# Outputs kept in 32 bits and stored through SyncE's queue instead of GpSimd's casting queue

## Chip, cores and metric

One core of a Trainium2 chip runs the whole program. The metric is the device time of one execution in microseconds (us), the median over runs; lower is better.

## What is computed

Dilated and sliding-window attention over 8 batches of 576 rows and 8 heads of 64, followed by a soft mixture of experts with 32 slots (8 experts, 4 slots each):

```python
scores = scale * np.matmul(q, k.transpose(0, 1, 3, 2))          # masked: window 32, or dilation 4
attn = np.exp(scores); attn = attn / attn.sum(-1)
x = np.matmul(attn, v)                                          # to rows [4608, 512]
logits = x @ phi                                                # [4608, 32]
d = np.exp(logits - logits.max(0)); d /= d.sum(0)
slot_input = d.T @ x
for e in range(E):
    h = np.maximum(slot_input[e] @ w1[e], 0.0)                  # 512 -> 1024
    slot_out[e] = h @ w2[e]                                     # 1024 -> 512
c = np.exp(logits - logits.max(1)); c /= c.sum(1)
return (c @ slot_out).astype(np.float32)                        # [4608, 512]
```

Inputs and the output are float32 in DRAM: q, k and v have 9.44 MB each, w1 and w2 16.8 MB each, the output 9.44 MB.

## The kernel before

All loads of inputs and weights go through GpSimd (POOL) as `nc.gpsimd.dma_start`, since they turn float32 into float16 on the way. The only transfer that SyncE (SP) issues is that of a small table of masks, `cst`. The order of instructions on each engine is the order in the source (`tc.manual_schedule()`).

**Attention.** A loop over the 8 batches, software-pipelined by an order written out by hand (`ORDER`), computes scores, exponentials, masks, outputs and logits. Each batch's q, k and v are loaded two batches ahead, and when the last batch has freed the buffers, the loads of w2 follow: experts 3 and 4 whole, then columns 0 to 255 of experts 5, 6 and 7 ("first half"), then their columns 256 to 511 ("second half"), two transfers for each half of an expert (`load_w2`, L207). These last twelve transfers each read 512 KB of DRAM in runs of 1 KB.

**Experts.** With all of w1 in place, the hidden layer is computed (L596 to L611), and then `emit_so` (L627) multiplies by w2 into the PSUM tile `so`, by halves of the columns for experts 5 to 7. `gather_so` (L642) and `spread_so` (L648) bring a finished half into `so_sb`.

**Output.** `emit_fin` computes 128 rows of the output: a matmul (L654) into PSUM, and a scaling by `rrow` on the way into the SBUF tile `om`, alternately on ScalarE (ACT, L663) and VectorE (DVE, L667). `emit_batch` does this for the four blocks of a batch and issues one store (L674). For six batches the first half of the columns is done and stored while the second half of w2 is still being loaded; between these come the `emit_so` of the second half:

```python
    for b in range(NHALF):                      # NHALF = 6
        if b in (2, 3, 5):
            emit_so(1, ({2: 5, 3: 6, 5: 7}[b],))
        if b == 5:
            gather_so(1)
        emit_batch(b, 0, DH)
    spread_so(1)
    for b in range(NHALF):
        emit_batch(b, DH, DMODEL)
    for b in range(NHALF, B):
        emit_batch(b, 0, DMODEL)
```

That gives six stores of half width (512 KB of float32 each, in runs of 1 KB), six more for the second half, two of full width (1 MB, runs of 2 KB), and at the end two stores (L701, 512 KB each, runs of 2 KB) of the rows 512 to 575 of all batches, out of the tile `om_l`. PE executes in order, so the first-half fins of batches 2, 3 and 5 stand behind the `emit_so` of experts 5, 6 and 7.

A program of this kind gives each outstanding transfer one of eight slots of its issuing engine; a later transfer in the same slot first waits for the earlier one to land.

Of the kernel before, what the change touches and what calls it, by code (L numbers as in the profile page):

```python
# [9 lines left out]
FP32 = mybir.dt.float32  # L10
FP16 = mybir.dt.float16
# [4 lines left out]
B = 8  # L16
# [8 lines left out]
DMODEL = H * D  # L25
# [71 lines left out]
def kernel(  # L97
# [10 lines left out]
    nc = tc.nc  # L108
# [25 lines left out]
    w1_pool = ctx.enter_context(tc.tile_pool(name="w1p", bufs=1))  # L134
    w2a_pool = ctx.enter_context(tc.tile_pool(name="w2a", bufs=1))
# [234 lines left out]
    def et_cols(b):  # L370
        base = 384 * (b // 2)
        return (base, base + 128) if b % 2 == 0 else (base + 256, base + 192)
# [154 lines left out]
    for it in range(B + max(s for _, s in STEPS)):  # L527
        for op, stage in STEPS:
            b = it - stage
# [28 lines left out]
    h_pool = tc.alloc_tile_pool(name="hp", bufs=1)  # L558
# [55 lines left out]
    psum_e.release()  # L614
    psum_f = tc.alloc_tile_pool(name="psum_f", bufs=4, space=bass.MemoryType.PSUM)

    om = [w1_pool.tile([128, 4, DMODEL], FP16, name=f"om_{b}", tag=f"w1_{b}") for b in range(B)]
    om_l = h_pool.tile([128, B // 2, DMODEL], FP16, name="om_l", tag="om_l")
    so = psum_so.tile([128, DMODEL], FP32, name="so", tag="so")

    def emit_so(s, experts):
# [30 lines left out]
    def emit_fin(m, j, c0, c1, dst, blk):  # L652
        fp = psum_f.tile([128, DMODEL], FP32, name=f"f_{blk}_{c0}", tag="f")
        nc.tensor.matmul(  # L654
            fp[:, 0 : c1 - c0],
            ET[32 * j : 32 * j + 32, m : m + 128],
            so_sb[32 * j : 32 * j + 32, c0:c1],
            start=True,
            stop=True,
        )  # L660
        turn[0] += 1
        if turn[0] % 2:
            nc.scalar.activation(  # L663
                out=dst, in_=fp[:, 0 : c1 - c0], func=AF.Copy, scale=rrow[:, blk : blk + 1]
            )
        else:
            nc.vector.tensor_scalar(  # L667
                out=dst, in0=fp[:, 0 : c1 - c0], scalar1=rrow[:, blk : blk + 1], scalar2=None, op0=ALU.mult
            )

    def emit_batch(b, c0, c1):
        for j in range(4):
            emit_fin(et_cols(b)[0], j, c0, c1, om[b][:, j, c0:c1], 4 * b + j)
        nc.gpsimd.dma_start(  # L674
            out=out[S * b : S * b + 512].rearrange("(j p) d -> p j d", p=128)[:, :, c0:c1],
            in_=om[b][:, :, c0:c1],
        )
# [8 lines left out]
# [11 lines that stand above are left out]
# [1 line left out]
        emit_fin(et_cols(2 * pr)[1], pr, 0, DMODEL, om_l[:, pr, :], 4 * B + pr)  # L698
    rest = out.rearrange("(n e s) d -> n e s d", e=2, s=S)
    for e in range(2):  # L700
        nc.gpsimd.dma_start(  # L701
            out=rest[:, e, 512:576, :].rearrange("n i d -> i n d"), in_=om_l[64 * e : 64 * e + 64]
        )
    in_order.__exit__(None, None, None)
# [35 lines left out]
```

## Time and profile before

| | before |
|---|---|
| time, median of 3 runs | 179.43 us (179.11 to 179.47) |
| the profiled execution | 179.36 us, of which 177.5 us are the span from the first to the last instruction |
| busy: PE, DVE, ACT, POOL | 69%, 71%, 70%, 25% of the span |
| read from and written to DRAM | 62.07 MB and 9.44 MB |
| issues of `out_dram<-om` | 12 of 512 KB, 2 of 1024 KB, all from POOL |
| issues of `out_dram<-om_l` | 2 of 512 KB, from POOL |

The profile describes one execution. Its second part cuts the span into 40 slices and gives in tenths how busy each engine and the DMA engines were; "GB/s" counts the bytes as they are at the destination, so a load that turns float32 into float16 counts half of what it reads. The chain of waits is followed back from the last instruction to what released it.

### The profile page before, as it was taken

What the parts mean: (1) busy time and instruction counts of PE and PEld (TensorE: products, weight loads), DVE (VectorE), ACT (ScalarE), POOL (GpSimd) and SP (SyncE); (2) the same over time, 40 slices, a digit from 0 to 9 for tenths busy, and PEclk for the clock granted to TensorE, in tenths of its full rate; (3) what the DMA queues carried; (4) which work ended last, traced back from release to release, by engine and by line L of the source; (5) the groups of instructions that cost most, each with busy time, mean ns of one, the idle gap of its engine ahead of it and who ended that gap; (6) DMA issues with size and microseconds to landing.
All of it is one profiled execution on the core that took longest, in us unless ns stands there. A gap on an engine that the chain in (4) does not pass through costs nothing.

```text
span 177.5 us, 4765 instructions
## 1 busy us (share of the span) xinstructions
PE 122.4 (69%) x2016; PEld 79.8 (45%) x2016; DVE 126.3 (71%) x277; ACT 123.8 (70%) x268; POOL 44.5 (25%) x70
## 2 busy tenths in 40 slices
PE   0026828888888988989888988996776736688100
PEld 0015616656666657666666656764332312221000
DVE  6483999999999999799999998455131017789200
ACT  6007758999999999979999999995401117688100
POOL 7321022112112112118110005111111514556400
PEclk9999999999999997599999999789859975555555
DMA  5999999999999999999999999999999999999995
GB/s 90 211 214 211 214 212 215 215 213 217 214 213 216 212 215 212 212 216 216 216 211 215 214 215 223 211 220 220 209 216 190 196 197 224 387 347 394 405 414 142
DMA packets 21061, 40.85 MB, mean 230 GB/s; under 512 B 1328, under 2 KB 13744, under 8 KB 20400
## 3 DMA queue, kind: packets, MB, share of 16 engines
q0 software_dynamic: 20896, 40.41, 114.8%
q8 instruction: 16, 0.26, 0.5%
q1 hardware_dynamic: 144, 0.14, 0.3%
q14 instruction: 5, 0.04, 0.1%
HBM read 62.07 MB, written 9.44 MB: 403 GB/s over the span
## 4 chain that ended last, share of the span: by engine, by line
DMA 46%; ACT 23%; DVE 9%; PE 9%; POOL 4%; issue 3%; POOLq 0%; DVEq 0%; ACTq 0%
DMA w<-in_moe_w_dram 38%; DMA phi_raw<-in_moe_phi_dram 8%; ACT p L269 5%; ACT vX L240 5%; ACT xp L324 4%; PE f L654 3%; DVE qk L218 3%; DVE vT L218 3%; ACT om L663 2%; ACT xT L363 2%; PE rv L234 2%; ACT xT L365 2%; POOL w L193 2%; PE s L260 2%; ACT xd L324 1%
## 5 line engine op out<-in xcount | busy, mean ns | idle before, releaser
L269 ACT ACTIVATE p<-s 128x1920 f16<-128x1920 f32 (+1 forms) x24 | 44.5, 1854 | 10.3 <-PE s L260 10.2
L260 PE MATMUL s<-qk 32*128 32x128 f16 (+2 forms) x704 | 26.7, 295 | 18.9 <-DVE qk L218 12.0
L240 ACT COPY vX<-rv 128x768 f16<-128x768 f16 (+1 forms) x32 | 27.7, 944 | 1.7 <-PE rv L234 1.7
L324 ACT ACTIVATE xp<-o_P,rc_P 128x64 f16<-128x64 f32 x96 | 26.7, 503 | 2.5 <-DVE rc_P L315 2.5
L303 PEld LDWEIGHTS <-p 128*128 128x128 f16 (+1 forms) x480 | 22.4, 103 | 13.4 <-issue 3.9
L260 PEld LDWEIGHTS <-qk 32*128 32x128 f16 x704 | 17.3, 117 | 22.1 <-DVE qk L218 12.0
L280 DVE TENSOR_TENSOR p<-p,masks 128x1920 f16<-128x1920 f16 (+1 forms) x24 | 25.8, 1085 | 0.3
L218 DVE STREAM_TRANSPOSE qk<-rawQ 128x576 uint32<-128x576 uint32 x16 | 18.8, 1242 | 2.7 <-DMA rawQ<-in_q_dram 2.7
L234 PE MATMUL rv<-cst,vT 128*128 128x128 f16 x176 | 18.2, 250 | 3.1 <-DVE vT L218 1.8
L303 PE MATMUL o_P<-vX,p 128*128 128x65 f16 (+1 forms) x288 | 19.8, 204 | 0.7 <-DVE xd L328 0.2
L218 DVE STREAM_TRANSPOSE qk<-rawK 128x576 uint32<-128x576 uint32 x16 | 19.6, 1235 | 0.4 <-DMA rawK<-in_k_dram 0.4
L218 DVE STREAM_TRANSPOSE vT<-rawV 128x576 uint32<-128x576 uint32 x16 | 19.4, 1224 | 0.4 <-DMA rawV<-in_v_dram 0.4
L234 PEld LDWEIGHTS <-vT 128*128 128x128 f16 x176 | 13.8, 126 | 7.1 <-issue 3.7
L667 DVE TENSOR_SCALAR om<-f,rrow 128x256 f16<-128x256 f32 (+1 forms) x28 | 13.5, 518 | 3.7 <-PE f L654 2.2
L207 POOL DMA_DIRECT2D w<-in_moe_w_dram x12 | 8.9, 748 | 26.3 <-DMA w<-in_moe_w_dram 22.4
L663 ACT ACTIVATE om<-f,rrow 128x256 f16<-128x256 f32 (+1 forms) x28 | 12.8, 503 | 3.1 <-PE f L654 2.4
L654 PE MATMUL f<-so_sb,ET 32*128 32x256 f16 (+1 forms) x60 | 12.0, 420 | 3.8 <-ACT om L663 2.5
L674 POOL DMA_DIRECT2D out_dram<-om x14 | 10.4, 747 | 12.4 <-DVE om L667 7.0
L188 POOL DMA_DIRECT2D rawQ<-in_q_dram x8 | 5.1, 633 | 29.5 <-DVE rc_P L315 18.6
L363 ACT COPY xT<-rp 128x576 f16<-128x576 f16 x16 | 11.3, 876 | 1.1 <-PE rp L344 1.1
L303 PE MATMUL o_D<-vX,p 128*128 128x65 f16 x128 | 10.0, 204 | 2.5 <-DVE xp L328 1.4
L365 ACT COPY xT<-rd 128x576 f16<-128x576 f16 x16 | 10.6, 787 | 0.0
(83 smaller groups left out, 182.5 us busy)
## 6 DMA issues: line engine op xcount, KB each, us to landing
w<-in_moe_w_dram POOLq DMA_DIRECT2D x13, 1024.0 KB, 24.3
out_dram<-om POOLq DMA_DIRECT2D x12, 512.0 KB, 5.9
rawQ<-in_q_dram POOLq DMA_DIRECT2D x8, 576.0 KB, 12.6
rawK<-in_k_dram POOLq DMA_DIRECT2D x8, 576.0 KB, 11.3
rawV<-in_v_dram POOLq DMA_DIRECT2D x8, 576.0 KB, 11.4
w<-in_moe_w_dram POOLq DMA_DIRECT2D x12, 256.0 KB, 15.8
out_dram<-om POOLq DMA_DIRECT2D x2, 1024.0 KB, 8.5
out_dram<-om_l POOLq DMA_DIRECT2D x2, 512.0 KB, 9.1
```

The lines of the kernel that those rows point to most:

```text
L218: nc.vector.transpose(out=out_, in_=in_)
L234: nc.tensor.transpose(rg[:, n_t, :, c, :], rows, ident)
L240: copy(out=vX[b % 2][:, t0 : t0 + n, :, 0:D], in_=rg.rearrange("p n h c d -> p n h (c d)"))
L260: nc.tensor.matmul(sps[:, h, c0 : c0 + w], kk, qq, start=(tt == 0), stop=(tt == 1))
L269: return nc.scalar.activation(out=pt, in_=sps[:, :, 0:n], func=AF.Exp, scale=SCALE)
L280: return nc.vector.tensor_tensor(out=pt, in0=pt, in1=m, op=ALU.mult)
L303: nc.tensor.matmul(o[rows, h, :], lhs, rhs, start=(n == 0), stop=(n == len(jobs) - 1), skip_group_check=True,)
L324: nc.scalar.activation(out=dst[:, h], in_=src[:, h], func=AF.Copy, scale=rc[:, h : h + 1])
L363: copy(out=xT_t[b][:, c, :], in_=rg[:, 0:S])
L365: copy(out=xT_t[b][:, 2 + c, :].rearrange("p (i r) -> p i r", r=DIL), in_=rg[:, :, 0:SUB].rearrange("p r i -> p i r"),)
L654: nc.tensor.matmul(fp[:, 0 : c1 - c0], ET[32 * j : 32 * j + 32, m : m + 128], so_sb[32 * j : 32 * j + 32, c0:c1], start=True, stop=True,)
L663: nc.scalar.activation(out=dst, in_=fp[:, 0 : c1 - c0], func=AF.Copy, scale=rrow[:, blk : blk + 1])
```

## The change

The SBUF tiles `om` and `om_l` become float32; `om_l` takes the place of expert 0's w2 instead of one of its own. The stores then need no cast and are issued by SP (`nc.sync.dma_start`). The program as built has the same instructions in the same order on PE, ACT and DVE, but for one more wait each on ACT and DVE ahead of the first write to `om_l` (for expert 0's w2 to have been loaded). The 16 stores, each with its wait for ACT and DVE, move from the end of POOL's stream to SP's, behind the load of `cst`. SP's closing waits, ahead of the end of the program, grow from five to nine.

```diff
-    om = [w1_pool.tile([128, 4, DMODEL], FP16, name=f"om_{b}", tag=f"w1_{b}") for b in range(B)]
-    om_l = h_pool.tile([128, B // 2, DMODEL], FP16, name="om_l", tag="om_l")
+    om = [w1_pool.tile([128, 4, DMODEL], FP32, name=f"om_{b}", tag=f"w1_{b}") for b in range(B)]
+    om_l = w2a_pool.tile([128, B // 2, DMODEL], FP32, name="om_l", tag="w2_0")
...
     def emit_batch(b, c0, c1):
         for j in range(4):
             emit_fin(et_cols(b)[0], j, c0, c1, om[b][:, j, c0:c1], 4 * b + j)
-        nc.gpsimd.dma_start(
+        nc.sync.dma_start(
             out=out[S * b : S * b + 512].rearrange("(j p) d -> p j d", p=128)[:, :, c0:c1],
             in_=om[b][:, :, c0:c1],
         )
...
     for e in range(2):
-        nc.gpsimd.dma_start(
+        nc.sync.dma_start(
             out=rest[:, e, 512:576, :].rearrange("n i d -> i n d"), in_=om_l[64 * e : 64 * e + 64]
         )
```

## The prediction

> **What bounds the kernel.** I read the page first, its 40 slices above all:
>
> ```profile
> PE 122.4 (69%) x2016; PEld 79.8 (45%) x2016; DVE 126.3 (71%) x277; ACT 123.8 (70%) x268; POOL 44.5 (25%) x70
> DMA  5999999999999999999999999999999999999995
> GB/s 90 211 214 211 214 212 215 215 213 217 214 213 216 212 215 212 212 216 216 216 211 215 214 215 223 211 220 220 209 216 190 196 197 224 387 347 394 405 414 142
> DMA 46%; ACT 23%; DVE 9%; PE 9%; POOL 4%; issue 3%; POOLq 0%; DVEq 0%; ACTq 0%
> ```
>
> No compute engine is above 71%, while the DMA engines are busy in every slice. Loads run at about 214 GB/s counted in float16, that is 428 GB/s of float32 read; stores at 390 to 414 GB/s of float32 written. The chain of waits ends in the weights:
>
> ```profile
> 83.91 32.72 DMA w<-in_moe_w_dram
> 116.91 24.54 DMA w<-in_moe_w_dram
> 141.73 10.43 DMA w<-in_moe_w_dram
> 152.20 0.43 PE so L627 x3
> ```
>
> The change is in what follows, so I next took the stretches from 142 us on (after the name of the stretch and its length, busy time with instructions of PE, PEld, DVE, ACT, POOL, then clock, DMA share, GB/s):
>
> ```profile
> 142.00:148.00 6.00, 2.67 (x26) 1.06 (x25) 1.99 (x6) 2.00 (x6) 0.50 (x2) 0.67 1.45 196
> 148.00:152.20 4.20, 2.98 (x33) 0.84 (x25) 2.97 (x7) 2.73 (x7) 2.74 (x4) 0.50 1.65 276
> 152.20:160.20 8.00, 5.86 (x35) 1.88 (x35) 6.17 (x15) 6.25 (x16) 4.56 (x7) 0.50 1.84 370
> 160.20:168.50 8.30, 4.11 (x13) 0.64 (x10) 4.85 (x8) 3.96 (x7) 4.38 (x7) 0.50 1.88 400
> ```
>
> and POOL's timeline (start, length, what, wait before it):
>
> ```profile
> 141.73 0.74 POOL L207 DMA_DIRECT2D w<-in_moe_w_dram  x1 [0.58 <-DMA w<-in_moe_w_dram]
> 147.97 0.75 POOL L674 DMA_DIRECT2D out_dram<-om  x1 [5.50 <-DVE om L667]
> ...
> 154.41 0.75 POOL L674 DMA_DIRECT2D out_dram<-om  x1 [1.04 <-ACT so_sb L648]
> 157.36 3.79 POOL L674 DMA_DIRECT2D out_dram<-om  x5 [2.21 <-ACT om L663]
> ...
> 165.97 1.27 POOL L701 DMA_DIRECT2D out_dram<-om_l  x2 [0.64 <-issue]
> ```
>
> Every store is issued by 167.2, yet the trace's completion marks (16 for each transfer, one per DMA engine) say that the last lands at 176.03: nine us of stores are queued when compute ends. The marks also show two groups of engines. The last weights land at 149.58 on the first engine and at 152.16 on the last. On the slow group the marks follow each other without a hole: six first-half stores land from 153.51 to 160.20 (1.32 to 1.39 us apart), the second half from 161.46 to 168.45, the full ones at 170.98 and 173.52, `om_l` at 174.78 and 176.03. So the end is the slow engines' work, one queue, weights before stores. The last store's landing is followed by 1.5 us of closing waits.
>
> **The change part by part.**
>
> *Scaling into float32.* The 256-column forms took 473 ns on ACT and 480 on DVE, the 512-column forms 686 and 748, all from float32 PSUM. If the wider write doubled the part that grows with columns (213 and 268 ns per 256), a batch's two on each engine would cost 0.5 us more, 1.5 in place of 1.0, over the 1.31 of a store; I take zero, since DVE's 268 ns for 256 columns is one column a cycle or so, set by what it reads, and the nine us of queued stores cover what is left.
>
> *POOL loses 16 issues* (0.75 us each, 10.4 + 1.3 us). They are its last work; the last load was issued at 141.73, so nothing stands behind them: nothing gained. *SP gains them.* It is idle from 1.1 us on, and only the closing waits stand behind them. The slot waits in its stream (first-half stores none, the others for a transfer eight places earlier) have been met long before. The two added waits on ACT and DVE are for a load of long ago: some 0.03 us, hidden.
>
> *Rate.* A store's packets are runs of 1 KB: 32 per engine in 1.31 us, 41 ns each; full width 2.53 us for 32 of 2 KB, 79 ns. Loads with 1 KB read and 512 bytes written come 1.32 us apart too, so the larger side of the packet sets the price, and a store whose two sides are 1 KB should cost what it costs now. The only row for SP's queue is `cst`, 128 runs of 1,096 bytes that follow each other at 46 ns on an engine; by the two prices above (38 ns per KB and 3 more) they would take 44. So 0 to 2 ns more for each of the 480 packets an engine has: 0 to 0.96 us, all on the path. I take 0, because an uncast 8 KB packet in the trace took 322 ns and a load's packet with 8 KB read 324.
>
> *Issue.* `cst` occupied SP for 0.34 us with 128 runs, and its engines finished over 0.38 us, so runs seem to be handed out one engine after the other. A store has 512 runs: 0.34 us if the cost is fixed, 1.36 if it goes with the runs, 0.68 for `om_l` (256 runs). I take a value under 1.31 us, where the DMA still sets the pace; the upper end is a rival below.
>
> *Order.* This is the real difference. Before, the first store waits behind all weights; now it has a queue of its own and runs beside the last of them. Batch 0's output is complete at 147.42 (DVE's mark). Call L the time from there to its packets on a slow engine (`cst`: 0.94 us from issue to first packet). Weights left there then: 152.16 - 147.42 - L = 4.74 - L. If both queues get equal turns, this takes twice as long, and the weights end 4.74 - L later. The second half's first output was complete at 155.59, 3.43 us after the last weights; now at 155.59 + 4.74 - L, and its packets start L later: at 160.33 whatever L is. Before, they started at 161.46 - 1.31 = 160.15. First-half work fills the time until then: the sum of weights and stores to 160.20 is unchanged, and batch 5 (153.89 + 4.74 = 158.63 with its L) arrives before its turn, 160.20 - 1.32 = 158.88. So the cost is 0.18 us. It is zero if the loads get the larger share, and grows if the stores do. After that compute delivers a batch each 0.96 us against 1.31 for its store, so the queue fills again; the slip of up to 3.8 us in compute is under the 9 us of cover.
>
> The trace of before has no stretch with both queues loaded, so the share is unknown. The Trainium skill ("DMA: Bandwidth & Descriptors", Queues, rings and completion order) says that each engine goes round its queues packet by packet, a packet holding several descriptors; no run here shows it yet. By that rule the sum would be the 0.18 us or, where a load's packet holds more than a store's, nothing.
>
> *End.* SP's closing waits start 0.065 us apart (176.08, 176.15, 176.21); up to five more now follow the last landing, +0.33. But before, the end waited for POOL's closing drain until 176.77, 0.49 us after SP was ready at 176.28. If that drain waits for POOL's own stores, it is now early and the end gains 0.16; if not, SP's later 176.61 still hides under it: 0. I take 0.
>
> Sum against the profiled execution: 179.36 + 0.18 = 179.54, so 179.5 us. That execution lies 0.07 under the median of 179.43. About 0.2%, 0.36 us, is what a measurement of this kernel can tell from no change.
>
> **The rivals.**
>
> *SP's issue becomes the pace (slower).* If handing out 512 runs takes 1.36 us and each wait some 0.05, six second-half stores come at 1.41 instead of 1.31: +0.6 us; with the packets' 2 ns on top up to +1.6: 180.1 to 181.1. It decides from 1.31 us per issue on. For it: the spread of `cst`'s engines. Against: it is one short row at the start of the program.
>
> *The stores take more than their share (slower).* If they always went first, the stores of batches 0 to 2 (4.0 us) would go ahead of the 3.5 us of weights left at 148.6 (L = 1.2); batch 3 stands behind expert 6's weights on PE and comes too late to push in. The weights would end at 156.1 and the second half's packets start at 156.1 + 3.43 + 1.2 = 160.7: +0.6, 180.0. With batch 3's 1.32 ahead as well it would be +1.9, 181.2.
>
> *GpSimd's queue has hitches that go (faster).* The second-half store of batch 0 began 1.7 us after its outputs, where the others took 0.5; and one engine landed batch 2 1.77 us after batch 1 instead of 1.31, 0.45 that it never made up (175.64 against 176.03 at the end). Without that and with POOL's drain gone: -0.39 - 0.16, 178.8. Against: POOL's issues took 746 to 755 ns without exception, the late one lay under a backlog until 160.20, and a 16 KB packet of instructions at 161.93 fits the hitch and would stay. The Trainium skill ("SBUF — State Buffer", The single rule) has a rule that would make it so: VectorE in some modes locks GpSimd out of writing descriptors, which SP's queue avoids. The trace's constant issue times do not bear it out here.
>
> **How the numbers follow.** The forecast (equal or smaller share for the stores, DMA's pace kept) has 0.42, by its unknown packet price split into same 0.31, slower 0.08, faster 0.03; its own range is 179.2 to 180.0. SP's pace or dearer packets 0.27; greedy stores 0.13; hitches gone 0.14; the rest, 0.04, same or slower. Faster 0.17, same 0.33, slower 0.50. The range runs from the faster rival to the upper end of the first: 178.8 to 181.1.
>
> **What would show it.** Right: the last landing at about 176.2, stores 1.31 and 2.53 us apart, last weights (the last `so` of L627) 2 to 4 us later than 152.2, `om` rows at 470 to 480 ns. Wrong: SP's store rows near or above 1.3 us, a DMA slice under 380 GB/s between 161 and 168 us, `om` rows over 650 ns, or SP's stores landing before any weight moves on.

## The result

The changed kernel takes 180.84 us (median of 5 runs, 180.76 to 181.24) against 179.43 (179.11 to 179.59): ratio 1.0089, 95% interval 1.0074 to 1.0103, so slower by 1.4 us. Timed again on the chip of the later experiments it had 1.0095 (1.0079 to 1.0110). The profiled execution took 181.24 us with a span of 179.4, against 179.36 and 177.5 before.

From the page of the changed kernel, the DMA row, the moved bytes, the queues, and the issues with the median time to landing:

```profile
DMA  5999999999999999999999999999999999999994
GB/s 87 211 214 210 218 211 213 215 212 217 216 213 217 211 216 212 214 216 214 214 215 215 214 216 225 214 214 221 210 208 192 197 196 270 373 366 355 381 338 143
q0 software_dynamic: 12960, 30.97, 89.9%
q1 hardware_dynamic: 8080, 9.58, 15.6%
...
out_dram<-om SPq DMA_DIRECT2D x12, 512.0 KB, 6.5
...
out_dram<-om SPq DMA_DIRECT2D x2, 1024.0 KB, 8.5
out_dram<-om_l SPq DMA_DIRECT2D x2, 512.0 KB, 9.6
```

The loads are as before up to slice 33. The stores, which ran at 387 to 414 GB/s (347 in one slice), now run at 355 to 381, and the slice before the last, 414 before, has 338. The same stretches as in the prediction, with the end cut finer (columns as there):

```profile
152.20:160.20 8.00, 5.14 (x33) 1.61 (x34) 5.38 (x14) 5.38 (x15) 0.00 (x0) 0.50 1.06 370
160.20:168.50 8.30, 5.16 (x18) 0.95 (x16) 6.16 (x11) 5.25 (x10) 0.00 (x0) 0.50 1.05 362
168.50:172.00 3.50, 0.00 (x0) 0.00 (x0) 0.00 (x0) 0.00 (x0) 0.00 (x0) 0.50 1.04 397
172.00:174.00 2.00, 0.00 (x0) 0.00 (x0) 0.00 (x0) 0.00 (x0) 0.00 (x0) 0.50 1.02 347
174.00:176.00 2.00, 0.00 (x0) 0.00 (x0) 0.00 (x0) 0.00 (x0) 0.00 (x0) 0.50 0.95 241
176.00:178.00 2.00, 0.00 (x0) 0.00 (x0) 0.00 (x0) 0.00 (x0) 0.00 (x0) 0.50 0.56 173
```

and three of these in the kernel before:

```profile
168.50:172.00 3.50, 0.00 (x0) 0.00 (x0) 0.00 (x0) 0.00 (x0) 0.00 (x0) 0.50 1.47 413
172.00:174.00 2.00, 0.00 (x0) 0.00 (x0) 0.00 (x0) 0.00 (x0) 0.00 (x0) 0.50 1.48 416
174.00:176.00 2.00, 0.00 (x0) 0.00 (x0) 0.00 (x0) 0.00 (x0) 0.00 (x0) 0.50 0.45 122
```

Two things are to be seen. The DMA share (the time of all packets over 16 engines) fell from 1.88 to 1.05 where the half-width stores run (160.2 to 168.5): before, nearly two packets of an engine were in flight at once on average, now one. And from 172 us on, where only a full-width store and then `om_l` are left, the rate falls to 347 and 241 GB/s with the engines still busy (share 1.02 and 0.95). In slices of 1 us from 140 us on, the stores run at 352 to 401 GB/s from 152 to 173 us, and the three slices from 174 to 177 us have 213, 268 and 260:

```profile
GB/s 195 213 185 195 196 197 195 196 197 223 291 323 371 373 374 376 369 365 373 367 361 361 357 352 359 352 362 373 389 401 393 399 391 303 213 268 260 86 0 0
```

The completion marks in the trace show where it adds up (landing on the last engine, us; "changed, again" is the run e0_after_again below):

| | before | changed | changed, again | e6_oml_all_parts |
|---|---|---|---|---|
| last weights | 152.16 | 153.55 | 153.49 | 152.95 |
| sixth first-half store | 160.20 | 161.08 | 160.95 | 160.43 |
| sixth second-half store | 168.45 | 169.37 | 169.15 | 168.61 |
| second full-width store | 173.52 | 174.48 | 174.25 | 173.74 |
| last of `om_l` | 176.03 | 178.03 | 177.78 | 176.31 |
| end of the span | 177.5 | 179.4 | 179.1 | 177.5 |

What follows the last full store took 2.51 us and takes 3.55 and 3.53: 1.0 us of the loss lies in the two `om_l` stores, 1 MB of 9.4. The rest, 0.7 to 1.0, is there by the sixth first-half store. Of this, 0.43 to 0.55 is older than any store: the fourth load from the end landed at 148.10 before and at 148.65 and 148.53 in the two traces of the changed kernel, ahead of the first packet in SP's queue (149.37 and 149.20). Up to there both kernels do the same. In the other kernels below in which SP stores `om` this load landed from 148.04 to 148.41, in those in which GpSimd does, from 148.00 to 148.71, so as far as these traces show this lag goes with the execution and not with the change.

### The profile page after: what moved, and what is told of

Read it like the earlier page. It is cut to its first block, busy times and chain, and to the rows that moved or that the text cites. A ratio compares the mean times of both kernels' runs of the same rounds, so it can differ in the third digit from the quotient of the medians.

```text
span 179.4 us, 4771 instructions
## 1 busy us (share of the span) xinstructions
PE 123.2 (69%) x2016; PEld 80.8 (45%) x2016; DVE 126.4 (70%) x277; ACT 123.8 (69%) x268; POOL 32.7 (18%) x54
## 4 chain that ended last, share of the span: by engine, by line
ACT 37%; DMA 30%; DVE 13%; PE 8%; issue 3%; POOL 2%; POOLq 0%; DVEq 0%; ACTq 0%
DMA w<-in_moe_w_dram 22%; ACT p L269 11%; DMA phi_raw<-in_moe_phi_dram 8%; ACT vX L240 7%; ACT xp L324 7%; DVE qk L218 5%; PE f L654 3%; ACT xT L363 3%; ACT xT L365 3%; DVE p L280 3%; DVE vT L218 3%; ACT om L663 2%; ACT xd L324 2%; PE s L260 2%; PE rv L234 1%
## 5 line engine op out<-in xcount | busy, mean ns | idle before, releaser
L269 ACT ACTIVATE p<-s 128x1920 f16<-128x1920 f32 (+1 forms) x24 | 43.9, 1831 | 10.7 <-PE s L260 10.6
L260 PE MATMUL s<-qk 32*128 32x160 f16 (+2 forms) x704 | 26.7, 295 | 18.7 <-DVE qk L218 12.4
L303 PEld LDWEIGHTS <-p 128*128 128x128 f16 (+1 forms) x480 | 23.2, 105 | 13.4 <-DVE xp L328 4.4
L240 ACT COPY vX<-rv 128x768 f16<-128x768 f16 (+1 forms) x32 | 27.2, 918 | 1.7 <-PE rv L234 1.7
L324 ACT ACTIVATE xp<-o_P,rc_P 128x64 f16<-128x64 f32 x96 | 25.9, 471 | 2.2 <-DVE rc_P L315 2.2
L303 PE MATMUL o_P<-vX,p 128*128 128x65 f16 (+1 forms) x288 | 20.6, 209 | 0.7 <-DVE xd L328 0.2
L667 DVE TENSOR_SCALAR om<-f,rrow 128x256 f32<-128x256 f32 (+1 forms) x28 | 13.5, 519 | 3.9 <-PE f L654 2.4
L663 ACT ACTIVATE om<-f,rrow 128x256 f32<-128x256 f32 (+1 forms) x28 | 12.8, 503 | 3.3 <-PE f L654 2.6
L328 DVE TENSOR_TENSOR xd<-o_D,rc_D 128x256 f16<-128x256 f32 x24 | 10.0, 415 | 0.2
```

The costliest lines, as they stand in the source:

```text
L240: copy(out=vX[b % 2][:, t0 : t0 + n, :, 0:D], in_=rg.rearrange("p n h c d -> p n h (c d)"))
L260: nc.tensor.matmul(sps[:, h, c0 : c0 + w], kk, qq, start=(tt == 0), stop=(tt == 1))
L269: return nc.scalar.activation(out=pt, in_=sps[:, :, 0:n], func=AF.Exp, scale=SCALE)
L303: nc.tensor.matmul(o[rows, h, :], lhs, rhs, start=(n == 0), stop=(n == len(jobs) - 1), skip_group_check=True,)
L324: nc.scalar.activation(out=dst[:, h], in_=src[:, h], func=AF.Copy, scale=rc[:, h : h + 1])
L663: nc.scalar.activation(out=dst, in_=fp[:, 0 : c1 - c0], func=AF.Copy, scale=rrow[:, blk : blk + 1])
```

## Experiments

**Theory P: half the partitions.** Each `om_l` store reads 64 of the 128 partitions; in 16 bits this was 256 KB for 512 KB written, now it is 512 KB, and reads of 64 partitions are limited to somewhere near the 213 to 268 GB/s of the last slices of about 1 us. **Rival Q: the queue.** SP's queue handles a packet dearer, everywhere alike.

### e1_oml_cast

```diff
-    om_l = w2a_pool.tile([128, B // 2, DMODEL], FP32, name="om_l", tag="w2_0")
+    om_l = h_pool.tile([128, B // 2, DMODEL], FP16, name="om_l", tag="om_l")
...
-        nc.sync.dma_start(out=rest[:, e, 512:576, :] ...
+        nc.gpsimd.dma_start(out=rest[:, e, 512:576, :] ...
```

> The changed kernel, with om_l alone back in 16 bits on GpSimd's casting queue. Theory P (half the partitions): the two om_l stores read 64 partitions each, and 32-bit reads of 64 partitions are limited near the 213 to 268 GB/s of the last slices; their excess, 178.03 - 174.48 = 3.55 us against 2.51, is most of the loss. Then 180.84 - 1.04 = 179.8 us, and the om_l pair lands 2.5 us after the last full store. Rival Q (SP's queue as such, packets one at a time at 44 ns instead of 41, SP held 0.8 to 1.4 us by an issue): om_l has 32 of 480 packets an engine, so 180.6 or more.

Measured: 182.01 us, ratio 1.0138 (1.0116 to 1.0160) to the kernel before in the same runs (179.62). A miss for both in time. In its trace, span 180.0, `om_l` has landed by 177.02, 0.8 to 1.0 earlier than in the two traces of the changed kernel, which is the direction that P gave, but not the clean test that P expected: GpSimd's packets ran beside SP's second full store, which landed late, at 175.77, and `om_l` only 1.25 behind it. From the first full store (171.57) to the last landing it took 5.45 us, between the 5.05 of the kernel before and the 6.11 of the changed one. The end then came 2.95 us after the last landing instead of 1.34. POOL's closing drain (a `DRAIN` instruction behind POOL's last issue, which the end of the program waits for) ended at 179.19, 2.17 us after POOL's last landing, while SP had finished its own closing waits, and so was ready to end, at 177.39.

### e2_oml_f32_pool

The changed kernel with `nc.gpsimd` in place of `nc.sync` for `om_l` alone, the tile staying FP32.

> The changed kernel, with om_l in 32 bits but stored through GpSimd's queue. P: width and partitions are what costs, so the pair still takes 3.4 us or more and the time stays near 180.8. Q: the queue is what costs, so the pair is back at 2.5 us and the time at 179.8.

Measured: 183.22 us, 1.0218 (1.0196 to 1.0241), again a miss for both in time. The last full store landed at 177.47, beside `om_l`, and `om_l` at 178.44: from the first full store (171.61) to the last landing 6.83 us, where the changed kernel took 6.11 and the kernel before 5.05. So `om_l` in 32 bits is dear in GpSimd's queue too, against Q; the end again came 2.95 us later, with POOL's drain.

### e3_all_f32_pool

All outputs FP32, both `dma_start` back on `nc.gpsimd`.

> All outputs in 32 bits, all stores through GpSimd's queue as before: the width alone. P: half-width stores 1.31 us apart as before, the om_l pair 1.0 us dearer: 180.4. Q: as before, 179.4. If uncast 1 KB packets are dearer in any queue: over 180.8.

Measured: 184.29 us, 1.0258 (1.0237 to 1.0280), dearer than either theory said; only the third line of the expectation, uncast packets dearer in any queue, holds. The stretch of half-width stores and the last ones:

```profile
160.20:168.50 8.30, 4.56 (x15) 0.74 (x12) 5.47 (x9) 4.57 (x8) 5.05 (x8) 0.50 1.00 317
...
174.00:176.00 2.00, 0.00 (x0) 0.00 (x0) 0.00 (x0) 0.00 (x0) 0.00 (x0) 0.50 1.06 262
176.00:178.00 2.00, 0.00 (x0) 0.00 (x0) 0.00 (x0) 0.00 (x0) 0.00 (x0) 0.50 0.96 178
```

The queue is that of before, and still the share is 1.00 and the rate 317 GB/s, under SP's 362. That one packet at a time is in flight comes from the missing cast, not from the queue: Q falls. Here the trace has packets of 4,096 bytes (four runs of 1 KB, or two of 2 KB, joined), 173 to 193 ns each in the median of the stretches up to 176 us, and 320 from 176 to 178, where `om_l` was read beside the rest of the last full store.

### e4_oml_two_queues

```diff
-        nc.sync.dma_start(
+        (nc.sync, nc.scalar)[e].dma_start(
```

> The changed kernel, with om_l's second store issued by ACT, so that the two stores, which read partitions 0 to 63 and 64 to 127, are in flight together. P: both halves are read at once, the pair takes about 2.5 us: 179.8. The Trainium skill (SBUF - State Buffer, Can I just issue two DMAs to hit both halves?) says that two such transfers serialize, with 6% gained: by it 180.6 to 180.8. Q: 180.7 to 180.8.

Measured: 181.74 us, 1.0124 (1.0107 to 1.0142), no better than the changed kernel's 1.0089 (1.0095 when timed again). ACT's store did not run beside SP's: it went ahead, beside the full store (landed by 176.03), and SP's, behind that full store (176.75), was left alone to the end at 178.41. So this does not test P. It agrees with the sentence of the Trainium skill that its expectation names only in that nothing was gained.

### e6_oml_all_parts, beside e0_after_again

The rows of `om_l` are interleaved, so that partition 2i + e holds row i of batch parity e, and a store covers all partitions. The permuted copy runs on ACT at 128.4 us for 0.7 us, when ACT is otherwise idle.

```diff
+    nc.scalar.copy(
+        out=ETl.rearrange("p r (i e) -> p r i e", e=2),
+        in_=ET.rearrange("p (r c) -> p r c", c=384)[:, :, 128:256].rearrange("p r (e i) -> p r i e", e=2),
+    )
...
-    for e in range(2):
+    for n in range(B // 2):
         nc.sync.dma_start(
-            out=rest[:, e, 512:576, :].rearrange("n i d -> i n d"), in_=om_l[64 * e : 64 * e + 64]
+            out=rest[n, :, 512:576, :].rearrange("e i d -> i e d"), in_=om_l[:, n, :]
```

> The changed kernel, with the rows of om_l interleaved (batch parity inside, row outside, by a permuted copy of those columns of ET), so that its 1 MB leaves in four stores of 256 KB that each read all 128 partitions, on SP in 32 bits as before. P (half the partitions): what follows the last full store takes 2.6 us as in the kernel before the change, not 3.55; 1.0 us under the changed kernel run beside it. Q (the queue alone): within 0.2 us of the changed kernel.

> The changed kernel once more, on the chip of the others: 180.8 us.

Measured: 179.72 us, 1.0024 (1.0016 to 1.0033), beside 180.94 for the changed kernel on the same chip: 1.2 us less. After the last full store `om_l` takes 2.57 us (173.74 to 176.31) in place of 3.53. (The profiled execution was the fastest of its eleven, 179.29, so its other marks stand early.)

```profile
160.20:168.50 8.30, 4.74 (x15) 0.81 (x14) 5.64 (x9) 4.74 (x8) 0.00 (x0) 0.50 1.06 369
168.50:172.00 3.50, 0.00 (x0) 0.00 (x0) 0.00 (x0) 0.00 (x0) 0.00 (x0) 0.50 1.04 397
172.00:174.00 2.00, 0.00 (x0) 0.00 (x0) 0.00 (x0) 0.00 (x0) 0.00 (x0) 0.50 1.05 395
174.00:176.00 2.00, 0.00 (x0) 0.00 (x0) 0.00 (x0) 0.00 (x0) 0.00 (x0) 0.50 0.71 268
```

The same bytes, width and queue keep 395 GB/s from 172 to 174 us, where the changed kernel fell to 347; in the next two microseconds this stream runs out (share 0.71), where the changed kernel was still busy at 241. With the control e7_before_layout below, in which this layout and its four stores alone change nothing, P is shown. The Trainium skill has this rule ("SBUF — State Buffer", Door 1: The DMA port swizzle): partitions 0 to 63 reach half of the DMA ports, for about 218 GB/s. The slices of the changed kernel in which `om_l` was read, 213 to 268 GB/s (219 to 297 in its second trace), lie near it and mostly above; that 218 is the limit here is not shown. The kernel before read about 200 GB/s there to write 400, which does not speak against it.

### e5_only_oml

The kernel before, with the change of `om_l` alone (FP32, `nc.sync`), the other 14 stores cast on GpSimd.

> The kernel before, with the change of om_l alone (32 bits, SP). P: the last 1 MB costs 1.0 us more than before as long as SP's first store waits its turn; since it has a queue of its own and runs beside the full stores of GpSimd's queue, part may be covered: 179.8 to 180.5. Q: 32 of 480 packets, 0.1 us: 179.5 to 179.6. POOL's closing drain was seen to end 2.2 us after its last landing in two runs; here its stores end earlier, so it should not show.

Measured: 178.80 us, 0.9974 (0.9966 to 0.9983): faster than the kernel before, by 0.5 us, where P said slower and Q no faster. The end of its stream:

```profile
168.50:172.00 3.50, 0.00 (x0) 0.00 (x0) 0.00 (x0) 0.00 (x0) 0.00 (x0) 0.50 1.41 406
172.00:174.00 2.00, 0.00 (x0) 0.00 (x0) 0.00 (x0) 0.00 (x0) 0.00 (x0) 0.50 1.19 393
174.00:176.00 2.00, 0.00 (x0) 0.00 (x0) 0.00 (x0) 0.00 (x0) 0.00 (x0) 0.50 0.44 164
```

Though issued at 165.5, SP's packets begin at 170 and run between the cast ones of the full stores; the reads of 64 partitions are covered there (393 GB/s where the changed kernel has 347), and the last landing is at 176.17, 0.14 after that of before. The gain is behind it: POOL's last store landed at 175.29 and its drain ended at 175.95, before SP was ready at 176.32, so the span ends 0.87 us after the last landing, not 1.47.

### e7_before_layout, e8_oml_sp_all_parts, e9_half_oml_sp

The interleaved layout on the kernel before: with all four stores cast on GpSimd, with all four in 32 bits on SP, and with two of each.

> The kernel before with the interleaved rows of om_l and their four stores, cast on GpSimd's queue: a control. P and Q: as before within 0.2 us, 179.4 to 179.6, since reads of 16 bits from 64 partitions were no limit (2.5 us for the pair).

> The kernel before, with om_l alone in 32 bits on SP (as in e5_only_oml), in the interleaved layout whose four stores read all 128 partitions. If e5_only_oml gained because POOL's closing drain (0.49 us after SP was ready in the kernel before) ends under SP's last stores, and the reads of 64 partitions were already covered by the stores of GpSimd's queue beside them, this one stands within 0.2 us of it: 178.7 to 178.9 us. If the reads of 64 partitions still cost there, it is 0.3 us or more under it: 178.5 or less. If the gain of e5_only_oml was a difference between chips or days, 179.3.

> The kernel before in the interleaved layout of om_l, with two of its four stores cast on GpSimd's queue and the two others in 32 bits on SP. In e5_only_oml SP's stores landed last (176.17) and the end followed 0.83 us later; in e8_oml_sp_all_parts GpSimd's landed last (176.84) and it took 1.46. If who lands last decides (POOL's closing drain is then hidden or not): 178.8 to 178.9 us if SP's land last by 0.5 us or more, 179.3 or more if GpSimd's do. If the drain is not the reason, 179.3 either way.

Measured: 179.26 us, 1.0000 (0.9991 to 1.0009); 179.90, 1.0031 (1.0019 to 1.0044); 179.58, 1.0009 (0.9998 to 1.0021). The layout itself costs nothing. e8_oml_sp_all_parts is a miss for all three lines of its expectation: its first `om_l` store was issued at 164.34, ahead of the second full one (164.88), and SP's then ran beside it, so that GpSimd's full store landed last, at 176.84, and the end followed 1.42 later. (The 0.83 and 1.46 in the expectation of e9_half_oml_sp should be 0.87 and 1.42.) In e9_half_oml_sp GpSimd's landed last too (176.58, SP's 175.30), end 1.49 later, as its expectation said for that case. The closing fits who lands last:

| | POOL's last landing | SP's last | POOL's drain ends | SP ready | end after last landing |
|---|---|---|---|---|---|
| before | 176.03 | | 176.77 | 176.28 | 1.47 |
| changed | 153.55 | 178.03 | 155.64 | 178.60 | 1.34 |
| e1_oml_cast | 177.02 | 175.77 | 179.19 | 177.39 | 2.95 |
| e5_only_oml | 175.29 | 176.17 | 175.95 | 176.32 | 0.87 |
| e9_half_oml_sp | 176.58 | 175.30 | 177.32 | 176.83 | 1.49 |

The kernels not in the table agree: 1.42 to 1.53 us after the last landing where POOL's is last and GpSimd stores `om` (e3, e7, e8), 2.95 where it is last and SP stores `om` (e2), 1.21 to 1.34 where SP's is last (e4, e6, e0). That e5_only_oml takes only 0.87 fits too: SP has one closing wait left to run after the last landing, where the changed kernel has eight, 0.06 us apart. No kernel was timed that alters the drain alone, so that the gain of e5_only_oml is the hidden drain rests on its trace and this table.

## Why the prediction was right or wrong

The forecast of no change, 179.5, with its own range of 179.2 to 180.0, was wrong; 180.84 lies in the wider range, and the slower side had been given 0.50. That is luck as far as the largest cost goes: no term and no rival stood for the 1.0 us of `om_l`, and the range reached up to 181.1 through SP's pace and 2 ns a packet together. The trace refutes the pace, and dearer packets alone were given no more than 0.96 us. Two of its signs of being wrong did appear: a DMA slice under 380 GB/s between 161 and 168 us (355), and rows of SP up to 1.38 us, which cost nothing (see *Issue*). What holds: the stores are the end, compute is covered, and `om` in 32 bits costs ACT and DVE nothing:

```profile
L667 DVE TENSOR_SCALAR om<-f,rrow 128x256 f32<-128x256 f32 x24 | 10.6, 481 | 3.6 <-PE f L654 2.3 <-DMA w<-in_moe_w_dram 0.8
L663 ACT ACTIVATE om<-f,rrow 128x256 f32<-128x256 f32 x24 | 10.2, 473 | 2.9 <-PE f L654 2.3
```

*Rate* is the step that failed, twice. First, it priced packets by their larger side and gave `om_l` its old 1.25 us a store, without asking from how many partitions a store reads: 1.0 us, 3.53 to 3.55 for the pair in place of 2.51, and 2.57 when all partitions are read. The question was there to be asked: the profile before has `out_dram<-om_l` x2 of 512 KB, and the code gives each of the two 64 partitions. A rule of the Trainium skill, cited above, would have raised it.

Second, it took nothing of its own 0 to 2 ns a packet. By the rates of the stretches of half-width stores, 16 x 1,024 bytes / 400 GB/s = 41 ns against 16 x 1,024 / 362 = 45, 4 ns more over all engines. On the last engine, which sets the end, most marks of half-width stores stand 1.35 to 1.38 us apart instead of 1.31 to 1.33, over 32 packets 1 to 2 ns more, inside the range that was given. The packet of 8 KB that was taken to prove zero was of the kind "instruction" in another queue (q14), no store; `cst`'s 46 ns, the one row for SP's queue, was the better guide. Little of this reached the end: from the first to the twelfth half-width store the last engine took 14.94 us before and 15.12 and 14.98 in the changed kernel, because before, one late engine had already lost 0.45 at one mark.

e6_oml_all_parts keeps the packets and the order, and is 0.43 us slower than the kernel before in the median. Its profiled execution is as fast as that of the kernel before, so how these 0.43 divide is not settled.

*Issue.* Right value, and the rival built on it falls:

```profile
L674 SPq DMA_DIRECT2D out_dram<-om x14: 372/375/1226, 147.9 to 165.5; - x14
...
L701 SPq DMA_DIRECT2D out_dram<-om_l x2: 899/1139/1379, 166.9 to 167.8; - x2
```

512 runs cost 372 ns, `cst`'s 128 runs 339: the cost hardly goes with the runs. The issues of over 480 ns all come after 160.3, with four or more stores still to land, and cost nothing.

*Order.* The 0.18 us was not seen, and the sharing was not as modelled. Equal turns from the start would have put the last weights 3 us later; they came 1.3 to 1.4 later (153.55 and 153.49), 0.4 to 0.55 of that from loads before any store. SP's first packets began at 149.20 to 149.42 in all six traces in which SP stores `om`, whether the store had been issued at 147.07 or at 147.91, about when the first engine came to the end of its loads (its last mark: 149.50 to 149.78). On the last engine, the load before the last still landed 1.33 and 1.41 us after its predecessor, and only the last one took 2.17 and 2.21. So the engines mostly finished the loads that were queued and then took the stores. The sixth first-half store and the first of the second half landed 1.35 and 1.38 us apart, with no hole. The greedy rival falls with it.

*End.* POOL's drain did go from the path, and SP's added waits came: 1.34 in both traces against 1.47, between the two values that were weighed. The faster rival's other half, the one late engine, was not recovered: the changed kernel has a 16 KB packet of instructions at 164.30, as the kernel before at 161.93, and one mark comes late behind it, 1.61 us after the one ahead, as 1.77 before.

## What to carry to other kernels

When a store loses its cast, work out what it reads as well as what it writes, and from how many partitions: a 64-partition source that cost nothing at 2 bytes an element cost 1.0 us for 1 MB at 4. A queue that needs less work from its engine is no gain where the DMA engines are the bound; ask instead how packets go through them. If GpSimd's stores are the last thing in a program, try to let another queue's land after them: moving just `om_l` gave 178.80 us, the best version here. It has to come out so in the trace: in e8_oml_sp_all_parts and e9_half_oml_sp GpSimd's stores still landed last, and nothing was gained.

## What was not expected of the hardware

- Casting stores had nearly two packets of an engine in flight (share 1.88, 400 GB/s in runs of 1 KB), uncast ones one (1.05 and 362 GB/s on SP's queue, 1.00 and 317 on GpSimd's). In runs of 2 KB SP's came to 397 (share 1.04), against 413 before (share 1.47).
- POOL's closing drain ended 0.66 to 0.82 us after POOL's last landing where GpSimd had issued the stores of `om`, and 2.09 to 2.17 after it where it had not. Why is open.
- A store that SP issued beside a backlog in GpSimd's queue began late: 1.5 to 2.3 us after its issue beside the weights, over 4 us (165.5 to 170) beside the stores of e5_only_oml, where `cst`, with nothing beside it, took 0.94.
